# Plain float32 in chunk 0's output product and chunk 1's P times V, w_out split one chunk later, other buffers and load order

## The chip, the cores and the metric

One Trainium2 chip, one of its cores. The metric is device microseconds of one launch on that core: the median of the runs, and beside it one execution under the hardware profiler.

## What is computed

Three layers one after the other, in float32. Sliding-window attention with a distance bias (4 sequences of 576 tokens, 8 heads of 64), a gated layer without activation, and a routed layer in which each of 2304 tokens goes to one of 8 experts:

```python
scores = scale * q @ k.T + bias          # window 128, causal
x = softmax(scores) @ v                  # then [2304, 512]
x = (x @ w_a) * (x @ w_b) @ w_out        # d_ff 1536
logits = x @ w_gate + modality_bias[modality_id]
e = argmax(logits); g = softmax(logits)[e]
out = g * (relu(x @ w1[e]) @ w2[e])
```

q and k are scaled up by about 5.3 and 5.4 and the gate's weights by 8. moe_w_a, moe_w_b and moe_w_out arrive as float64; the kernel reads their two 32-bit words and makes a float32 out of them with three bit operations on VectorE (DVE).

## The kernel before

Tokens are cut into 18 tiles of 128, grouped in seven chunks of 3, 2, 2, 3, 3, 3 and 2 tiles (`CH`, line 33). The gated layer runs chunk by chunk; within a chunk it takes 12 steps j, one for each 128 columns of d_ff. A step makes two products of 24 instructions (`mm_ab`, line 489), multiplies them into `gf` on DVE, and one step later adds the output product (`mm_out`, line 505) for each tile of the chunk into three PSUM banks. While chunk c runs, attention for chunk c+1 is worked off between its products, an item being one tile of one pair of heads; a pair's loads are issued by `a_load` (line 141) and its operands made by `a_prep_q`, `a_prep_k`, `a_prep_v`.

Most products are split: each float32 operand is held as a rounded part and a remainder (type float32r), made by one cast on ScalarE (ACT) and one subtraction on DVE, and three terms replace one product. Plain float32 is used where `S32` (scores of chunks 0 and 1) and `V32` (probabilities times V, chunk 0) say so. With plain float32 the normalisation of the probabilities is put off to the eviction of the product (`pv_ev`), and the result must be turned by a transpose (`pv_tr`); the split form (`pv6_mm`) gives it turned already.

Chunk 0 has an order written out by hand. Its attention runs first (lines 739 to 832, under `manual_schedule`), with the float64 conversion of weight blocks 0 and 1 in between (`conv_step`). Then `slot0` (line 954) is one step of chunk 0 together with the conversion of block j+2 of w_a and w_b, of block j+1 of w_out, and with chunk 1's attention items. In it `wo_jobs` converts a w_out block, splits it and writes the split to DRAM (`wo_d`, line 481); all later chunks fetch that back (`wo_fetch`, line 485). Outside the hand-made part a planner orders each engine's instructions by priority and by its own model of when they are ready, SP's queue of transfers included.

Routing of a chunk's tokens happens in the first steps of the next: `rd_fetch` loads gate rows, `rd_dot` makes dot products on DVE, `rd_fin` writes the rows to `x2d`. `x2_init` (line 846) fills the rows of `x2d` that are not routed yet with zeros. After chunk 6 the experts run.

Buffers are rings named by tag: `asb` (two), `gf` (one), `g` (two), `wo` (four), `x2` (three), `x2T` (one).

Of the kernel before, what the change touches and what calls it, by code (L numbers as in the profile page):

```python
# [21 lines left out]
def attn_moe_moe2(ctx: ExitStack, tc, q, k, v, moe_w_a, moe_w_b, moe_w_out, modality_id,  # L22
# [39 lines left out]
    CJ = 3  # L62
    CA = 1
    QPB = 1
    EVD = 1
    PJ = 5
    KDE = (1,)
    V6 = (1, 2, 3, 4, 5, 6)
    S32 = (0, 1)
    V32 = (0,)  # L70

    const = ctx.enter_context(tc.tile_pool(name="const", bufs=1))
    rt = ctx.enter_context(tc.tile_pool(name="rt", bufs=2))
# [261 lines left out]
                                 start=(b == 0), stop=(b == 1))  # L335

    def pv_ev(it):
        it.o = at.tile([P, 2, D], F32, tag="uy"[(it.a.hp * it.a.nt + it.t) % 2], bufs=1, name="u")
        for h in range(2):
            if it.a.c == 0 and EVD:  # L340
                nc.vector.tensor_scalar(out=it.o[:, h], in0=it.po[:, h, 0:D],
                                        scalar1=it.mx[:, 6 + h:7 + h], scalar2=None, op0=ALU.mult)
                continue
            nc.scalar.activation(out=it.o[:, h], in_=it.po[:, h, 0:D], func=AF.Copy,
                                 scale=it.mx[:, 6 + h:7 + h])
# [77 lines left out]
    def f64_ops(rv, key, put):  # L423
        st = []

        def one():
            f = m1.tile([P, 4 * P], U32, name="f64f", **(dict(tag="x2T", bufs=1) if key == "o" else dict(tag="x2", bufs=X2B)))
            st.append(f)
            nc.vector.tensor_scalar(out=f, in0=rv[:, :, 1], scalar1=3, scalar2=0x3FFFFFFF,
                                    op0=ALU.logical_shift_left, op1=ALU.bitwise_and)  # L430

        def two():
            nc.vector.scalar_tensor_tensor(out=st[0], in0=rv[:, :, 1], scalar=0xC0000000, in1=st[0],  # L433
                                           op0=ALU.bitwise_and, op1=ALU.bitwise_or)
# [30 lines left out]
    WOQ = 0  # L465
    WOB = 4
    wo_d = dram.tile([NJ, P, 2, DM], F32, name="wo_d")
    wo_t = {}

    def wo_load(j):  # L470
        r = m1.tile([P, DM, 2], U32, tag="wo", bufs=WOB, name="wor")
        nc.sync.dma_start(out=r.rearrange("p a b -> p (a b)"), in_=moe_w_out.bitcast(U32)[j * P:(j + 1) * P, :])
        wraw["o", j] = r

    def wo_jobs(j):
        fs = []

        def sp():
            wo_t[j] = m1.tile([P, 2, DM], F32R, tag="wo", bufs=WOB, name="wo")
            f64_split(fs[0], wo_t[j], nc.vector)  # L480
            nc.sync.dma_start(out=wo_d[j], in_=wo_t[j].bitcast(F32))

        return f64_ops(wraw.pop(("o", j)), "o", fs) + [("s", sp)]

    def wo_fetch(j):
        wo_t[j] = m1.tile([P, 2, DM], F32R, tag="wo", bufs=WOB, name="wo")
        (nc.scalar if WOQ else nc.sync).dma_start(out=wo_t[j].bitcast(F32), in_=wo_d[j])

    def mm_ab(c, j, m, part=None):
        n = CH[c] * P  # L490
# [197 lines left out]
    def consts_load():  # L688
        nc.sync.dma_start(out=wg, in_=w_gate.rearrange("(k p) e -> p k e", p=P))
        nc.sync.dma_start(out=mb.rearrange("p m e -> p (m e)"),  # L690
                          in_=modality_bias.rearrange("m (o e) -> o (m e)", o=1).partition_broadcast(P))
        mid_i = cl[0] = m1.tile([P, NT, 2], I32, tag="asb", bufs=2, name="mid_i")
        nc.sync.dma_start(out=mid_i.rearrange("p t w -> p (t w)").rearrange("p (t w) -> p t w", w=2),
                          in_=modality_id.bitcast(I32).rearrange("(t p w) -> p t w", p=P, w=2))

    def consts_ap():
        cl[1] = tinit = m1.tile([P, TI * TW], I32, tag="asb", name="tinit")
# [25 lines left out]
    def consts_b():  # L723
        mid = rt.tile([P, NT], F32, tag="vt", bufs=1, name="mid")
        nc.gpsimd.tensor_copy(out=mid, in_=cl[0][:, :, 0])
        tb = m1.tile([P, NT * (E + 2)], F32, tag="asb", name="tb")
# [11 lines left out]

    with tc.manual_schedule():
        if WU:  # L740
            wz = m1.tile([P, 2 * P], BF16, tag="asb", bufs=2, name="wz")
            nc.vector.memset(wz.bitcast(F32), 0.0)
            wps = ps_at.tile([P, 2 * P], F32, tag="att", name="ps_w")
            for _ in range(WU):
                nc.tensor.matmul(wps, lhsT=wz[:, 0:P], rhs=wz, start=True, stop=True)
        for h in range(H):
            nc.vector.memset(qscale[64 * (h % 2):64 * (h % 2) + 64, h // 2:h // 2 + 1], 0.125 * 2.0 ** (h + 1))
        new_xr(0)
        a_loads(n0 - 1)
# [91 lines left out]
    def upto(w, f, g):  # L841
        while cur[w] < min(g, len(items)):
            f(cur[w])
            cur[w] += 1

    def x2_init():
        zrow = m1.tile([P, DM + 1], F32, tag="x2", bufs=X2B, name="zrow")
        nc.gpsimd.memset(zrow, 0.0)
        for i in range(C0[NC - 2 if NC - 2 in RD else NC - 1], NT + 1):
            nc.sync.dma_start(out=x2d[i * P:(i + 1) * P, :], in_=zrow)  # L850
# [95 lines left out]

    queued = []

    hold = []

    def cum0(j):
        return ((j + 1) * NP * CH[1] + NJ - 1) // NJ

    def slot0(j):
# [10 lines left out]
                with tc.high_priority(offset=HP0):  # L965
                    a_pv(live.pop(g))

        dq(hold, "s")
        hold.clear()
        dq(jw[:4], "d")  # L970
        psa = mm_ab(c, j, 0, None if j else 1)
        asb = m1.tile([P, MT * P], F32, tag="asb", bufs=2, name="asb")
        nc.scalar.copy(out=asb[:, :n], in_=psa[:, :n])
        if act:
            c1, hp1, t1 = items[g + 2]
# [7 lines left out]
                score_inv(sg)  # L983
                score_nrm(sg)
        psb = mm_ab(c, j, 1)
        gf = m1.tile([P, MT * P], F32, tag="gf", bufs=1, name="gf")
        nc.vector.tensor_tensor(out=gf[:, :n], in0=psb[:, :n], in1=asb[:, :n], op=ALU.mult)
        if last:
            V()
            x_split(1)  # L990
        gt = m1.tile([P, 2, MT * P], F32R, tag="g", bufs=2, name="g")
        nc.scalar.copy(out=gt[:, 0, :n], in_=gf[:, :n])
        (nc.gpsimd if j in GLP else nc.vector).tensor_tensor(out=gt[:, 1, :n], in0=gf[:, :n], in1=gt[:, 0, :n], op=ALU.subtract)
        if act:
# [12 lines left out]
    pend = None
    for c in range(NC):
        n = CH[c] * P
        for j in range(NJ):  # L1010
# [21 lines left out]
            if c == NC - 1 and j == EJ:
                assert cur["o"] == len(items)
# [302 lines left out]
```

## Time and profile before

| | us |
|---|---|
| median of 3 runs | 855.36 (854.55 to 856.16) |
| the profiled execution | 856.61 |
| its span, first to last instruction | 854.9 |
| mean granted TensorE clock | 0.988 |
| TensorE busy (PE) | 812.0, 95% |
| weight loads busy (PEld) | 740.3, 87% |
| VectorE (DVE) / ScalarE (ACT) / GpSimd (POOL) | 570.6 / 437.7 / 187.8 |

Times in the rows are microseconds unless marked ns. PE's busy time includes the latency of pipelined instructions, so a busy PE need not be at its peak. SPq is SyncE's queue, which issues nearly all transfers, in order. A digit of the busy line is the busy share of one fortieth of the span in tenths.

### The profile page before, as it was taken

The page shows a single profiled execution, that of the slowest core. Times are in us where ns is not written, and L with a number is a line of the kernel's source. Part 1 is how long each engine was busy: PE and PEld are TensorE (multiplying, and loading weights), DVE is VectorE, ACT ScalarE, POOL GpSimd, SP SyncE. Part 2 cuts the span into 40 slices and gives each one's busy share as a digit, 9 for nine tenths or more (in the row PEclk, how much of TensorE's full clock was granted, in tenths as well). Part 3 has the DMA queues.
Part 4 walks back from the last instruction along what each step waited for, and adds up shares of the span by engine and source line. Part 5 has one row for each costly group of instructions (what it writes and reads, how often), then busy time and mean ns, then how long its engine had stood idle before and what let it go on. Part 6 is the DMA issues. An engine that isn't in the chain of part 4 may idle for free.

```text
span 854.9 us, 14384 instructions
## 1 busy us (share of the span) xinstructions
PE 812.0 (95%) x4806; PEld 740.3 (87%) x4806; DVE 570.6 (67%) x1732; ACT 437.7 (51%) x1153; POOL 187.8 (22%) x245
## 2 busy tenths in 40 slices
PE   7889877999999999999999999999999999999994
PEld 5779766889899989999999999999988998989893
DVE  6999999896796797557955594368375544447420
ACT  5756674653756766566546642232245443546420
POOL 4413214022122222221222121100033130114001
PEclk8989999999999999999999999999999999999998
DMA  9994434478876556343544244647328564549201
GB/s 268 355 405 160 132 103 142 174 233 220 192 220 193 155 152 203 111 127 95 173 142 131 69 139 137 185 148 236 98 102 303 200 196 137 169 127 303 99 32 39
DMA packets 66274, 145.50 MB, mean 170 GB/s; under 512 B 11951, under 2 KB 32079, under 8 KB 66192
## 3 DMA queue, kind: packets, MB, share of 16 engines
q1 hardware_dynamic: 62576, 134.64, 51.1%
q0 software_dynamic: 3616, 9.86, 3.3%
q8 instruction: 40, 0.66, 0.3%
q14 instruction: 42, 0.34, 0.1%
HBM read 125.63 MB, written 19.11 MB: 169 GB/s over the span
## 4 chain that ended last, share of the span: by engine, by line
PE 71%; issue 8%; DVE 7%; DMA 6%; ACT 4%; POOL 2%; SPq 1%; POOLq 0%; ACTq 0%; DVEq 0%
PE ps_ab L498 29%; PE acc L512 14%; PE ps_y L1088 8%; PE ps_h L1105 8%; PE ps_o L369 4%; PE ps_s L247 2%; DMA wraw<-in_moe_w_a 1%; PE ps_p L297 1%; DMA kr<-in_k 1%; PE ps_s L243 1%; DMA qr<-in_q 1%; POOL out L1095 1%; DMA wo<-wo_d 1%; DVE wab L445 1%; DVE f64f L433 1%
## 5 line engine op out<-in xcount | busy, mean ns | idle before, releaser
L498 PE MATMUL ps_ab<-xr,wab 128*128 128x384 f32 (+1 forms) x2016 | 339.6, 317 | 7.0 <-ACT asb L1049 1.9
L498 PEld LDWEIGHTS ps_ab<-xr,wab 128*128 128x128 f32 x2016 | 308.9, 189 | 19.1 <-ACT wab L444 4.5
L512 PE MATMUL acc<-wo,g 128*128 128x512 f32 x648 | 174.1, 399 | 4.9 <-DVE wo L445 2.0
L512 PEld LDWEIGHTS acc<-wo,g 128*128 128x128 f32 x648 | 115.5, 188 | 23.9 <-DVE wo L445 3.0
L311 POOL TENSOR_SCALAR_AFFINE_SELECT pt<-pc 128x512 fp32r<-128x512 f32 (+1 forms) x72 | 57.2, 794 | 322.8 <-DVE pc L309 215.9
L1088 PE MATMUL ps_y<-w2s,h 128*128 128x512 f32 x456 | 109.7, 394 | 0.0
L1105 PE MATMUL ps_h<-xT,w1s 128*128 128x384 f32 x576 | 104.1, 337 | 0.0
L1105 PEld LDWEIGHTS ps_h<-xT,w1s 128*128 128x128 f32 x576 | 99.7, 188 | 1.1 <-issue 0.5
L1088 PEld LDWEIGHTS ps_y<-w2s,h 128*128 128x128 f32 x456 | 84.2, 188 | 16.7
L579 DVE CUSTOM_DVE_ANT_0 junk<-x,wgt 128x512 f32<-128x512 f32 x128 | 91.5, 715 | 7.7 <-DMA wgt<-in_wgt 4.6
L271 ACT ACTIVATE p<-p,mx 128x128 f32<-128x128 f32 x144 | 56.7, 396 | 30.2 <-DVE mx L261 29.6
L1056 ACT CAST g<-gf 128x256 fp32r<-128x256 f32 (+1 forms) x72 | 33.1, 459 | 62.8 <-DVE gf L1053 61.0
L1049 ACT COPY asb<-ps_ab 128x256 f32<-128x256 f32 (+1 forms) x72 | 30.6, 425 | 65.0 <-PE ps_ab L498 64.5
L1053 DVE TENSOR_TENSOR gf<-ps_ab,asb 128x256 f32<-128x256 f32 (+1 forms) x72 | 35.0, 486 | 41.8 <-PE ps_ab L498 37.1
L369 PE MATMUL ps_o<-pt,vv 128*128 128x256 f32 x360 | 56.6, 290 | 1.7 <-POOL pt L311 1.1
L313 POOL TENSOR_SCALAR_AFFINE_SELECT pt<-pc 128x512 fp32r<-128x512 f32 (+1 forms) x72 | 57.1, 792 | 0.0
L862 DVE TENSOR_TENSOR w2s<-wr,w2s 128x1024 fp32r<-128x1024 f32 x24 | 29.4, 1226 | 39.7 <-ACT w2s L861 39.5
L369 PEld LDWEIGHTS ps_o<-pt,vv 128*128 128x128 f32 x360 | 50.0, 189 | 4.1 <-POOL pt L311 1.4
L862 DVE TENSOR_TENSOR w1s<-wr,w1s 128x1024 fp32r<-128x1024 f32 x28 | 34.3, 1225 | 24.0 <-ACT w1s L861 24.0
L1095 POOL DMA_INDIRECT out<-y,idx x19 | 22.8, 1203 | 119.9 <-ACT y L1094 118.1
L284 ACT ACTIVATE p<-p,mx 128x128 f32<-128x128 f32 x120 | 41.5, 394 | 13.0 <-DVE mx L276 12.2
L1108 ACT ACTIVATE h<-ps_h 128x384 fp32r<-128x384 f32 x48 | 23.5, 492 | 47.0 <-PE ps_h L1105 47.0
(204 smaller groups left out, 1066.0 us busy)
## 6 DMA issues: line engine op xcount, KB each, us to landing
wo<-wo_d SPq DMA_DIRECT2D x72, 512.0 KB, 3.8
wr<-in_moe_w SPq DMA_DIRECT2D x56, 512.0 KB, 4.1
wgt<-in_wgt SPq DMA_DIRECT2D x24, 512.0 KB, 4.2
wraw<-in_moe_w_a SPq DMA_DIRECT2D x12, 512.0 KB, 8.9
wraw<-in_moe_w_b SPq DMA_DIRECT2D x12, 512.0 KB, 8.2
wor<-in_moe_w_out SPq DMA_DIRECT2D x12, 512.0 KB, 4.8
wo_d<-wo SPq DMA_DIRECT2D x12, 512.0 KB, 2.8
kr<-in_k SPq DMA_DIRECT2D x24, 256.0 KB, 4.2
```

The costliest lines, as they stand in the source:

```text
L271: nc.scalar.activation(out=it.p[:, h, :], in_=it.p[:, h, :], func=AF.Exp, bias=it.mx[:, 2 + h:3 + h], scale=-1.0, accum_out=it.mx[:, 4 + h ...
L284: nc.scalar.activation(out=it.p[:, h, :], in_=it.p[:, h, :], func=AF.Copy, scale=it.mx[:, 6 + h:7 + h])
L311: nc.gpsimd.affine_select(out=it.pt[:, :, 0], in_=pc, pattern=pat + [[-1, P]], base=0, channel_multiplier=1, compare_op=ALU.is_gt, fill=0.0)
L313: nc.gpsimd.affine_select(out=it.pt[:, :, 1], in_=pc, pattern=pat + [[1, P]], base=0, channel_multiplier=-1, compare_op=ALU.is_ge, fill=0.0)
L369: nc.tensor.matmul(it.po, lhsT=a.vv[:, t + b, r].rearrange("p h d -> p (h d)"), rhs=it.pt[:, :, b, s, :], start=(i == 0), stop=(i == 5))
L498: nc.tensor.matmul(ps[:, :n], lhsT=w[:, m, r, kk * P:(kk + 1) * P], rhs=xr[:, s, kk, :n], start=(idx == 0), stop=(idx == len(terms) - 1))
L512: nc.tensor.matmul(acc[c, t], lhsT=g[:, r, t * P:(t + 1) * P], rhs=w[:, s, :], start=(j == 0 and idx == 0), stop=(j == NJ - 1 and idx == 2))
L579: nc.vector.tensor_tensor_reduce(out=junk, in0=x2[:, 0:DM], in1=wgt[:, k], scale=1.0, scalar=0.0, op0=ALU.mult, op1=ALU.add, accum_out=lgr ...
L862: nc.vector.tensor_tensor(out=dst[:, 1], in0=srcw, in1=dst[:, 0], op=ALU.subtract)
L1053: nc.vector.tensor_tensor(out=gf[:, :n], in0=psb[:, :n], in1=asb[:, :n], op=ALU.mult)
L1088: nc.tensor.matmul(pss[t], lhsT=h[:, r, f, t * P:(t + 1) * P], rhs=W2[f // 2][:, s_, f % 2, :], start=(f == 0 and i == 0), stop=(f == 7 an ...
L1105: nc.tensor.matmul(ps, lhsT=W1[f // 2][:, r, kk, (f % 2) * P:(f % 2 + 1) * P], rhs=xT[:, s_, kk, :], start=(kk == 0 and i == 0), stop=(kk ...
```

## The change

Chunk 0's output product takes `gf` and w_out as they are, in plain float32. So in chunk 0 the split of g and that of w_out go. The converted w_out block goes to DRAM as plain float32 (`wo_f`); chunk 1 fetches it from there, splits it (`wo_split`), uses it and writes the split to `wo_d` for the later chunks. `V32` takes chunk 1 in: its probabilities stay plain float32, are normalised at the eviction, and a transpose is added. In chunk 0's attention one of the two evictions of an item goes from DVE to ACT. In SP's order weight block 0 now stands ahead of pairs 2 and 3 of chunk 0. The zero rows are written one block per step from step 5 of chunk 3, instead of six at step 2 of chunk 1. Buffers: `asb` has one instead of two; the modality table is loaded into `gf`, the bias table's scratch lies in `x2T`; the attention output `u` lies in `g` or `x2T`; the float32 w_out block lies in `wo`.

```diff
-    V32 = (0,)
+    V32 = (0, 1)
     def pv_ev(it):
-        it.o = at.tile([P, 2, D], F32, tag="uy"[(it.a.hp * it.a.nt + it.t) % 2], bufs=1, name="u")
+        it.o = m1.tile([P, 2, D], F32, name="u", **(dict(tag="x2T", bufs=1) if it.a.c else dict(tag="g", bufs=2)))
         for h in range(2):
-            if it.a.c == 0 and EVD:
+            if it.a.c == 0 and h == 0:
                 nc.vector.tensor_scalar(out=it.o[:, h], in0=it.po[:, h, 0:D],
...
-            f = m1.tile([P, 4 * P], U32, name="f64f", **(dict(tag="x2T", bufs=1) if key == "o" else dict(tag="x2", bufs=X2B)))
+            f = m1.tile([P, 4 * P], U32, name="f64f", **(dict(tag="wo", bufs=WOB) if key == "o" else dict(tag="x2", bufs=X2B)))
...
+    class WoOps(list):
+        def append(self, f):
+            wo_t[self.j] = f
+            nc.sync.dma_start(out=wo_f[self.j], in_=f)
     def wo_jobs(j):
-        fs = []
-        def sp():
-            wo_t[j] = m1.tile([P, 2, DM], F32R, tag="wo", bufs=WOB, name="wo")
-            f64_split(fs[0], wo_t[j], nc.vector)
-            nc.sync.dma_start(out=wo_d[j], in_=wo_t[j].bitcast(F32))
-        return f64_ops(wraw.pop(("o", j)), "o", fs) + [("s", sp)]
+        return f64_ops(wraw.pop(("o", j)), "o", WoOps(j))
+    def wo_fetch(j, c):
+        if c > 1:
             wo_t[j] = m1.tile([P, 2, DM], F32R, tag="wo", bufs=WOB, name="wo")
+            nc.sync.dma_start(out=wo_t[j].bitcast(F32), in_=wo_d[j])
+        else:
+            wo_s[j] = at.tile([P, DM], F32, tag="wos", bufs=2, name="wos")
+            nc.sync.dma_start(out=wo_s[j], in_=wo_f[j])
+    def wo_split(j):
+        f, w = wo_s.pop(j), wo_t[j]
+        nc.scalar.copy(out=w[:, 0], in_=f)
+        nc.vector.tensor_tensor(out=w[:, 1], in0=f, in1=w[:, 0], op=ALU.subtract)
+        nc.sync.dma_start(out=wo_d[j], in_=w.bitcast(F32))
...
         for t in range(CH[c]):
+            if c == 0:
+                nc.tensor.matmul(acc[c, t], lhsT=g[:, t * P:(t + 1) * P], rhs=w, start=(j == 0), stop=(j == NJ - 1))
+                continue
...
-        a_loads(n0 - 1)
+        a_loads(CH[0])
         qq_zero(pairs[0, 0])
         make_masks(lambda: a_preps(0))
+        wab_load(0)
+        a_loads(n0 - 1)
         for hp_ in range(1, NP):
             qq_zero(pairs[0, hp_])
         consts_load()
-        wab_load(0)
...
     def slot0(j):
-        dq(hold, "s")
-        hold.clear()
-        asb = m1.tile([P, MT * P], F32, tag="asb", bufs=2, name="asb")
+        asb = m1.tile([P, MT * P], F32, tag="asb", bufs=1, name="asb")
-        gf = m1.tile([P, MT * P], F32, tag="gf", bufs=1, name="gf")
+        gf = m1.tile([P, MT * P], F32, tag="g", bufs=2, name="gf")
-        gt = m1.tile([P, 2, MT * P], F32R, tag="g", bufs=2, name="g")
-        nc.scalar.copy(out=gt[:, 0, :n], in_=gf[:, :n])
-        (nc.gpsimd if j in GLP else nc.vector).tensor_tensor(out=gt[:, 1, :n], in0=gf[:, :n], in1=gt[:, 0, :n], op=ALU.subtract)
+        if last:
+            wo_fetch(0, 1)
+            wo_fetch(1, 1)
-        return c, j, gt, wo_t[j]
+        return c, j, gf, wo_t[j]
...
-            if c == 1 and j == 2:
+            if c == 3 and (j == 5 or j > 5 and zr):
                 x2_init()
...
             upto('o', do_pv, g - OG)
+            if c == 1:
+                wo_split(j)
+                if j + 2 < NJ:
+                    wo_fetch(j + 2, c)
```

## Rows read from the trace of the kernel before

**Rows 1.** The page's busy tenths in 40 slices of the span, for VectorE.

```profile
DVE  6999999896796797557955594368375544447420
```

**Rows 2.** Table by stretch: length, busy time (instructions) by engine, clock, DMA share, GB/s.

```profile
0.00:45.60 45.60, 34.58 (x195) 28.29 (x196) 37.42 (x174) 27.47 (x93) 19.97 (x60) 0.90 0.99 318
45.60:159.40 113.80, 99.74 (x528) 87.76 (x529) 109.62 (x268) 67.01 (x183) 28.61 (x28) 0.98 0.52 177
159.40:223.70 64.30, 62.23 (x446) 57.23 (x446) 50.47 (x181) 35.58 (x110) 12.72 (x15) 1.00 0.79 223
```

**Rows 3.** The same table for 15.6 to 22.4 and for stretches of the slots.

```profile
15.60:22.40 6.80, 5.40 (x19) 4.76 (x20) 6.19 (x28) 2.90 (x9) 2.20 (x7) 0.50 1.02 399
...
45.60:55.30 9.70, 8.64 (x36) 7.58 (x36) 8.35 (x25) 4.51 (x13) 0.61 (x2) 0.79 1.03 398
55.30:87.50 32.20, 32.14 (x179) 29.95 (x180) 31.73 (x81) 20.30 (x59) 8.70 (x10) 1.00 0.63 222
87.50:145.80 58.30, 45.58 (x248) 38.56 (x246) 56.49 (x142) 36.84 (x102) 18.37 (x16) 1.00 0.43 136
```

**Rows 4.** VectorE's timeline in chunk 0's attention: start, length, instruction, idle before it.

```profile
16.04 0.43 DVE L429 TENSOR_SCALAR f64f<-wraw 128x512 uint32<-128x512 uint32 x1 [4.84 <-DMA wraw<-in_moe_w_a]
...
22.51 0.47 DVE L341 TENSOR_SCALAR u<-ps_o,mx 128x64 f32<-128x64 f32 x2
```

**Rows 5.** The chain of waits before 60 us: start, length, what.

```profile
9.98 6.04 DMA wraw<-in_moe_w_a
...
17.45 1.71 PE ps_s L243 x4
...
24.00 0.87 PE ps_s L243 x4
...
25.09 0.84 PE ps_o L334 x8
25.93 0.12 PE ps_ot L351
...
42.58 9.77 DMA qr<-in_q
```

**Rows 6.** The chain of waits of the whole span, three undisturbed groups of split products.

```profile
343.14 1.44 PE ps_o L369 x12
...
397.33 4.17 PE ps_ab L498 x24
401.51 2.10 PE acc L512 x9
```

**Rows 7.** Groups by line and shape, 45.6 to 159.4, VectorE: busy, mean ns, idle before.

```profile
L445 DVE TENSOR_TENSOR wo<-f64f,wo 128x512 fp32r<-128x512 f32 x10 | 7.6, 755 | 0.4 <-ACT wo L444 0.3
...
L993 DVE TENSOR_TENSOR g<-gf,g 128x384 fp32r<-128x384 f32 x11 | 6.0, 547 | 0.0
...
L309 DVE TENSOR_TENSOR pc<-ps_p,pc 128x256 fp32r<-128x256 f32 x12 | 4.9, 412 | 1.5 <-ACT pc L308 1.5
...
L226 DVE TENSOR_TENSOR vv<-vr,vv 128x384 fp32r<-128x384 f32 x6 | 3.7, 619 | 0.0
```

**Rows 8.** The same groups for TensorE's products.

```profile
L498 PE MATMUL ps_ab<-xr,wab 128*128 128x384 f32 x288 | 58.0, 350 | 4.6 <-ACT wab L444 1.7 <-DVE f64f L437 1.7 <-DVE wab L445 0.9
L512 PE MATMUL acc<-wo,g 128*128 128x512 f32 x99 | 26.6, 400 | 2.1 <-DVE wo L445 2.0
L369 PE MATMUL ps_o<-pt,vv 128*128 128x256 f32 x66 | 11.3, 299 | 1.7 <-POOL pt L311 1.1 <-DVE pc L309 0.6
L243 PE MATMUL ps_s<-kk,qq 128*128 128x256 f32 x28 | 7.6, 396 | 0.0
```

**Rows 9.** The table by stretch, first half of chunk 1.

```profile
159.40:192.60 33.20, 31.13 (x218) 28.15 (x218) 29.23 (x87) 20.53 (x60) 5.88 (x6) 1.00 0.71 227
```

**Rows 10.** What SP's queue waited for, whole span: us in total, times, longest.

```profile
SPq L481 <- DVE wo L445: 21.6, 7, 8.8
```

**Rows 11.** SP's timeline, 199 to 224: the zero rows' writes.

```profile
206.70 3.07 SPq L850 DMA_DIRECT2D x2d<-zrow  x6
```

**Rows 12.** The chain of waits, 180 to 240: a load of k.

```profile
221.76 10.10 DMA kr<-in_k
```

More of the change, by code (lines that the diff above doesn't have):

```diff
@@ L64, in attn_moe_moe2 @@
     QPB = 1
-    EVD = 1
     PJ = 5
@@ L467, in attn_moe_moe2 @@
     wo_d = dram.tile([NJ, P, 2, DM], F32, name="wo_d")
+    wo_f = dram.tile([NJ, P, DM], F32, name="wo_f")
     wo_t = {}
@@ L473, in wo_load, with __init__ @@
         wraw["o", j] = r
+    class WoOps(list):
+        def __init__(self, j):
+            self.j = j
+        def append(self, f):
+            wo_t[self.j] = f
+            nc.sync.dma_start(out=wo_f[self.j], in_=f)
     def wo_jobs(j):
-        fs = []
-        def sp():
+        return f64_ops(wraw.pop(("o", j)), "o", WoOps(j))
+    wo_s = {}
+    def wo_fetch(j, c):
+        if c > 1:
             wo_t[j] = m1.tile([P, 2, DM], F32R, tag="wo", bufs=WOB, name="wo")
-            f64_split(fs[0], wo_t[j], nc.vector)
-            nc.sync.dma_start(out=wo_d[j], in_=wo_t[j].bitcast(F32))
-        return f64_ops(wraw.pop(("o", j)), "o", fs) + [("s", sp)]
-    def wo_fetch(j):
-        wo_t[j] = m1.tile([P, 2, DM], F32R, tag="wo", bufs=WOB, name="wo")
-        (nc.scalar if WOQ else nc.sync).dma_start(out=wo_t[j].bitcast(F32), in_=wo_d[j])
+            nc.sync.dma_start(out=wo_t[j].bitcast(F32), in_=wo_d[j])
[7 more added lines that the diff above has]
+        nc.sync.dma_start(out=wo_d[j], in_=w.bitcast(F32))
     def mm_ab(c, j, m, part=None):
@@ L691, in consts_load @@
                           in_=modality_bias.rearrange("m (o e) -> o (m e)", o=1).partition_broadcast(P))
-        mid_i = cl[0] = m1.tile([P, NT, 2], I32, tag="asb", bufs=2, name="mid_i")
+        mid_i = cl[0] = m1.tile([P, NT, 2], I32, tag="gf", bufs=1, name="mid_i")
         nc.sync.dma_start(out=mid_i.rearrange("p t w -> p (t w)").rearrange("p (t w) -> p t w", w=2),
@@ L696, in consts_ap @@
     def consts_ap():
-        cl[1] = tinit = m1.tile([P, TI * TW], I32, tag="asb", name="tinit")
+        cl[1] = tinit = m1.tile([P, TI * TW], I32, tag="asb", bufs=1, name="tinit")
         nc.gpsimd.iota(tinit, pattern=[[0, TI * TW]], base=N, channel_multiplier=1)
@@ L725, in consts_b @@
         nc.gpsimd.tensor_copy(out=mid, in_=cl[0][:, :, 0])
-        tb = m1.tile([P, NT * (E + 2)], F32, tag="asb", name="tb")
+        tb = m1.tile([P, NT * (E + 2)], F32, tag="x2T", bufs=1, name="tb")
         mm1 = tb[:, 0:2 * NT].rearrange("p (m t) -> p m t", m=2)
@@ L740, in attn_moe_moe2 @@
         if WU:
-            wz = m1.tile([P, 2 * P], BF16, tag="asb", bufs=2, name="wz")
+            wz = m1.tile([P, 2 * P], BF16, tag="asb", bufs=1, name="wz")
             nc.vector.memset(wz.bitcast(F32), 0.0)
@@ L844, in upto @@
             cur[w] += 1
+    zr = []
     def x2_init():
[L847 to L850, printed above, removed]
+        if not zr:
+            zrow = m1.tile([P, DM + 1], F32, tag="x2", bufs=X2B, name="zrow")
+            nc.gpsimd.memset(zrow, 0.0)
+            zr.extend((zrow, i) for i in range(C0[NC - 2 if NC - 2 in RD else NC - 1], NT + 1))
+        zrow, i = zr.pop(0)
+        nc.sync.dma_start(out=x2d[i * P:(i + 1) * P, :], in_=zrow)
+        return bool(zr)
     SP = [mybir.EngineType.SP]
@@ L947, in attn_moe_moe2 @@
     queued = []
-    hold = []
     def cum0(j):
@@ L1003, in slot0 @@
         a_preps(n0 + cum0(j) + PJ - 1)
-        hold.extend(jo)
-        return c, j, gt, wo_t[j]
+        return c, j, gf, wo_t[j]
     pend = None
@@ L1024, in attn_moe_moe2 @@
                     wo_load(j + 2)
-            else:
-                wo_fetch(j)
+            elif c > 1:
+                wo_fetch(j, c)
             a_loads(g + (LD if c else LD0))
@@ L1047, in attn_moe_moe2 @@
             psa = mm_ab(c, j, 0)
-            asb = m1.tile([P, MT * P], F32, tag="asb", bufs=2, name="asb")
+            asb = m1.tile([P, MT * P], F32, tag="asb", bufs=1, name="asb")
             nc.scalar.copy(out=asb[:, :n], in_=psa[:, :n])
@@ L1059, in attn_moe_moe2 @@
                 mm_out(*pend)
+            if c == 1:
+                wo_t[j] = m1.tile([P, 2, DM], F32R, tag="wo", bufs=WOB, name="wo")
             pend = (c, j, gt, wo_t[j])
             upto('o', do_pv, g - OG)
+            if c == 1:
+                wo_split(j)
+                if j + 2 < NJ:
+                    wo_fetch(j + 2, c)
             a_preps(g + 1)
@@ L1197, in s_gather @@
     def s_gather(ov):
-        idx = m1.tile([P, 1], I32, tag="asb", bufs=2, name="idx")
+        idx = m1.tile([P, 1], I32, tag="asb", bufs=1, name="idx")
         nc.sync.dma_start(out=idx, in_=tab[bass.ds(ov, P), 0:1])
```

## The prediction

> **What bounds the kernel now.** I read the page first: VectorE (DVE) is full in the first eight fortieths of the span, and nearly idle later [rows 1]. A table by stage then gives the limits. Up to 45.6 us chunk 0's attention runs; from 45.6 to 159.4 us chunk 0's twelve expert slots, with chunk 1's attention between them; from 159.4 to 223.7 us chunk 1's twelve steps [rows 2]. In the slots DVE is busy 109.6 of 113.8 us (96%), TensorE (PE) 99.7 and ScalarE (ACT) 67.0. In chunk 1 PE is busy 62.2 of 64.3 and DVE 50.5.
>
> PE's busy time covers the pipeline's latency too, so I count its work by passes. On the undisturbed chain 24 products of 384 columns take 4.17 us (0.174 each), 9 of 512 columns 2.10 (0.234), 12 of 256 columns 1.44 (0.120) [rows 6]; these are split (fp32r) operands, one pass each. Plain float32 shows twice as many instructions as products: 4 of 256 columns in 0.87 us (0.217 each), 8 of 64 columns in 0.84 (0.105 each) [rows 5]. In the slots PE runs 288, 99, 66 and 28 of these four larger kinds [rows 8], and 47 more instructions (528 in all, rows 2) that I price at 0.12: 50.1 + 23.2 + 7.9 + 6.1 + 5.6 = 92.9 us in 113.8. So DVE is the limit of this stage, but not evenly. From 55.3 to 87.5 us both engines are full; from 87.5 to 145.8 DVE has 56.5 of 58.3 us, PE 45.6 [rows 3]. The first slot, 45.6 to 55.3, is limited by neither: the clock averages 0.79, and the DMA engines are at 1.03 [rows 3].
>
> In the attention before it DVE waits 4.84 us, until 16.04, for the first raw weight block; that transfer was issued only at 9.98 [rows 4, 5].
>
> **Start: block 0 loaded ahead of pairs 2 and 3.** Its two transfers move ahead of two pairs and three constants in SP's queue. Six loads of 192 KB stand before it instead of twelve and more, so it should land about when DVE first asks, at 11.2. Term: -4.8 (bounds 0, if the order does not come out so, and -4.8). From 15.6 to 22.4 us, right after the engines had stood still in that wait, the granted clock is 0.50, that is 1.2 instead of 2.4 GHz, and a score group takes 1.71 us instead of 0.87 [rows 3, 5]. The 6.8 us hold up to three such groups, 2.5 us dearer, but DVE is busy for 6.2 of them; I take -1.0 (0 to -2.5). Pairs 2 and 3 come later by 1 MB, at the 399 GB/s shown there 2.6 us; two pairs of work lie before them, so I take 0 (to +2.6).
>
> **Start: half of each eviction leaves DVE.** Two evictions take 0.47 us [rows 4]; one of two goes to ACT, 12 x 0.235 = 2.8, and chunk 1's first V split (0.6) goes. ACT has 18 us free here [rows 2]. Where a step is held by PE (0.87 + 0.84 and three transposes of 0.12 for an item, rows 5) the gain is hidden: I take -2.5 (0 to -3.4).
>
> **Start: what is late next.** The next late thing is visible: a load of q for chunk 1, issued at 42.58, lands at 52.34 and ends an ACT wait on the chain [rows 5], with the DMA engines full. The bytes ahead of it are nearly the same after the change. If its place in SP's order stays, it eats all that the start gains (8.3); if the planner moves it up with the step that frees its buffer, nothing. I take +2.5 (0 to +8.3), nearer to the second, because its buffer is freed by that step.
>
> **Slots: DVE.** Removed: 11 subtractions of g (6.0), 10 of w_out (7.6), 8 of the 12 on pc (chunk 1 has four pairs of two tiles; 8 x 0.412 = 3.3), 3 on vv (3 x 0.62 = 1.9) [rows 7]. 109.6 - 18.8 = 90.8. ACT loses the casts beside them and chunk 1's normalisation, and gains two small evictions and a copy per item; at 67.0 of 113.8 it hides them. GpSimd's selects take half the width, and cost nothing where hidden.
>
> **Slots: PE.** A plain float32 output product replaces three split ones. Its two instructions at 512 columns are not in the trace; from 0.217 at 256 columns I take 0.432 each: 0.864 against 3 x 0.234 = 0.702, or +0.162; 33 in this window, +5.3 us. Lower bound: two passes at the split price, 0.468, a gain of 7.7 us; excluded as a value, since 256 columns already cost 0.217 against 0.120. Upper bound: two passes at twice 0.234, 0.936, +7.7 us. P times V for chunk 1 becomes 8 passes (0.84) and a transpose (0.12) for 6 split ones (0.72): +0.24 an item, +1.9. PE: 92.9 + 5.3 + 1.9 = 100.1.
>
> At 256 columns a plain product takes 0.434, and four split passes would take 0.48 [rows 5, 6]. The Trainium skill (FP8 and Floating Point Precision, TensorE Precision Notes) counts true FP32 as 4 passes through the array, which speaks against this change, as the split needs 3. By that count a product at 512 columns would be 4 x 0.234 = 0.936, the slots 2.4 us longer and the forecast near 847; the trace agrees but for 10%, and I go by its row.
>
> **Slots: the sum.** DVE falls to 90.8, PE rises to 100.1: PE becomes the bound. The first slot's 36 instructions [rows 3] are 24 products, 8 plain score passes and 4 small ones, 6.1 us by the prices above; it loses 3.6 us beyond that, which I keep: 103.7. In the stretch from 87.5 DVE's 56.5 lose their share by time of the 18.8 (9.6), PE's 45.6 gain theirs of the 7.2 (3.7): 46.9 and 49.3, so the two are level and must wait for each other in turn; I add 1.8 for each, the idle that DVE shows there now: 107.3. Term: 113.8 to 107.3, -6.5 (-13.7 if PE's work alone counts; -0.9 if PE waits 0.7 at each of the eight new transposes, which need ACT's eviction first and hold the slot's products behind them).
>
> **Chunk 1.** The split of w_out comes here: an ACT copy (0.62) and a DVE subtraction (0.755 [rows 7]) per step, with a 512 KB write that SP issues only after the subtraction, and a 256 KB fetch in place of 512. Queued behind that write are the fetch for step j+2 and the k, q and v loads of the next chunk; the out-product of the next step waits for the subtraction. On ACT the copy waits for the fetch, with the next evictions and exponentials behind it. In the first half DVE is busy 29.2 of 33.2 [rows 9]: six more make 33.8, over the stretch by 0.6, and any delay comes in order. In the second half there is room. I take +2.5 (-1, as PE loses about 2 us now, to +7).
>
> **Zero rows.** Six writes of 256 KB leave 206.7 to 209.8 us, and 12 us later loads of k take 10.10 us [rows 11, 12]. One per step in chunk 3 costs nothing there. I take -1.0 (-2.6 to +0.5; the w_out writes put a net 3 MB into this chunk where the zero rows put 1.5). The single asb buffer waits for a product that the PSUM bank's next user awaits anyway: 0 (to +2). The bias table's scratch and the modality load: 0, as SP reaches that load long after the mask scratch it now shares is free.
>
> **Sum.** -4.8 - 1.0 - 2.5 + 2.5 - 6.5 + 2.5 - 1.0 = -10.8. The profiled execution took 856.61 us (span 854.9, 1.7 around it); 845.8 by the sum. The median of the runs is 855.36, 1.25 lower, so I forecast 844.6.
>
> **Rivals.** (a) The front is held by transfers, or the planner leaves SP's order as it is: the start's 8.3 are lost or eaten, 2.5 given back less. 844.6 + 5.8 = 850.4. For it: DMA share 0.99 up to 45.6 and 1.03 after it [rows 2, 3]. Against: up to 45.6 DVE idles 8.2 us, 4.84 of them in the one wait that the change attacks [rows 2, 4].
> (b) All covers hold: transfers move up with the prologue (-2.5), slots reach 103.7 (-3.6), chunk 1 absorbs the split (-2.5): 836.0. For it: DVE's room in chunk 1's second half. Against: both engines level.
> (c) Slower: chunk 1's split. SP holds the write of w_out until DVE subtracts, with loads behind it. In the slots that wait came 7 times in 12, 21.6 us in all, 3.1 each, at most 8.8 [rows 10]. If the subtraction falls behind routing's dot products in DVE's queue by more than a step (5.3 us), the next out-product, and PE, stand still. Six steps at 3.1, 18.6 in place of 2.5, give 860.7. It decides from five of the twelve steps on: 842.1 + 15.5 = 857.6. Against: PE lost only 2 us in that half so far.
> (d) The gains and the losses meet: PE's additions fall on the slots that are full now, with (a): about 855.
>
> **How the numbers follow.** A difference of 0.2% (1.7 us) is about what a measurement of this kernel can tell. Forecast, 839 to 850: 0.56. (a) 0.12; (b) 0.13; (c) 0.11; (d) 0.08. Range: from (b) with its bounds, 833, to 854.5, leaving out (c) and part of (d). Faster: forecast, (a) and (b), 0.81; same 0.07 and slower 0.12 from (d) and (c).
>
> **What would show it.** Right: no wait for wraw near 11 us; the attention ends near 38 to 40; slots of chunk 0 with PE above 95% and DVE below it; output products as two instructions of about 0.43 spacing; chunk 1 at 65 to 68 us; no 10 us loads near 220. Wrong: an ACT wait for q of over 5 us in slot 0; a pass near 0.47 or 0.23; PE idle in chunk 1 ended by the subtraction of w_out; PE idle before the transpose of chunk 1's outputs.

## The result and the profile after

The changed kernel takes 844.98 us (median of 4 runs, 843.65 to 846.12) against 855.76 for the kernel before beside it: 0.9872, interval 0.9846 to 0.9898. The forecast was 844.6. The profiled execution took 843.99 us with a span of 842.2, 12.7 less than before. By stage (a chunk begins with its first step product):

| us | start | chunk 0 slots | chunk 1 | 2 | 3 | 4 | 5 | 6 | rest |
|---|---|---|---|---|---|---|---|---|---|
| before | 45.6 | 113.7 | 64.4 | 68.6 | 96.9 | 92.9 | 82.5 | 52.2 | 238.0 |
| after | 41.2 | 102.4 | 64.2 | 68.6 | 98.7 | 93.8 | 82.8 | 52.2 | 238.3 |

The total came out as forecast; its parts did not. The start gave 4.4 us instead of 5.8, the slots 11.3 instead of 6.5, chunk 1 cost nothing instead of 2.5, and chunk 3, where the zero rows were to cost nothing, lost 1.8.

First the page's digits for VectorE in the kernel after, against [rows 1]: the full stretch at the front has holes.

```profile
DVE  8989995987875976658865683377376444447420
```

The table by stretch of the kernel after (length; busy us of PE, PEld, DVE, ACT, POOL with instructions; clock, DMA share, GB/s): the start, the slots, chunk 1, chunk 3; then the first slot alone and the inner part of the start. It answers [rows 2, 3].

```profile
0.00:41.20 41.20, 35.10 (x196) 26.63 (x196) 35.27 (x163) 28.54 (x101) 20.46 (x60) 0.98 0.96 295
41.20:143.60 102.40, 102.40 (x519) 84.62 (x519) 92.08 (x237) 53.60 (x158) 17.45 (x28) 0.98 0.61 211
143.60:207.80 64.20, 62.32 (x444) 56.77 (x443) 53.25 (x183) 39.91 (x112) 11.32 (x14) 1.00 0.70 219
276.40:375.10 98.70, 95.08 (x565) 88.50 (x564) 67.78 (x230) 61.01 (x183) 22.67 (x31) 1.00 0.59 156
...
41.20:51.10 9.90, 9.90 (x48) 9.16 (x47) 7.44 (x24) 3.87 (x12) 2.39 (x5) 0.75 1.02 409
16.00:38.00 22.00, 19.11 (x116) 14.50 (x115) 19.76 (x86) 17.37 (x65) 11.11 (x26) 1.00 1.03 336
```

In the slots PE is busy all 102.40 us, DVE 92.08: the bound has passed from DVE to PE. In chunk 3 PE stands idle for 3.6 us, where it was 1.4 before. From 16 to 38 us the granted clock is 1.00, where part of it was 0.50 before.

DVE's timeline of the kernel after at the point of [rows 4]: the first raw weight block now costs a wait of 0.61 us at 11.38, where it cost 4.84 at 16.04.

```profile
11.38 0.55 DVE L428 TENSOR_SCALAR f64f<-wraw 128x512 uint32<-128x512 uint32 x1 [0.61 <-DMA wraw<-in_moe_w_a]
```

The waits of the start after, of ACT and of PE (us in total, times, longest): the eviction given to ACT waits for DVE's half of the same result, and PE's transposes wait for ACT.

```profile
ACT u L343 <- DVE u L340: 6.1, 7, 1.3
...
PE ps_ot L350 <- ACT u L343: 1.5, 3, 0.8
```

Groups by line and shape after, 41.2 to 143.6 for PE and (last line) chunk 1 for DVE, against [rows 7, 8]: 66 instructions of the plain output product stand where 99 split ones stood, and the split of w_out is on DVE in chunk 1.

```profile
L511 PE MATMUL ps_ab<-xr,wab 128*128 128x384 f32 x288 | 62.5, 362 | 0.0
L524 PE MATMUL acc<-f64f,gf 128*128 128x512 f32 x66 | 30.8, 594 | 0.0
L242 PE MATMUL ps_s<-kk,qq 128*128 128x256 f32 x28 | 8.3, 412 | 0.0
L333 PE MATMUL ps_o<-vv,pt 128*128 128x64 f32 x64 | 8.3, 268 | 0.0
...
L499 DVE TENSOR_TENSOR wo<-wos,wo 128x512 fp32r<-128x512 f32 x11 | 7.6, 690 | 2.6 <-ACT wo L498 1.8 <-DMA wo_d<-wo 0.8
```

The chain of waits of the kernel after: four plain passes of 512 columns, and in chunk 3 a load of gate rows, which stands where [rows 12] had a load of k.

```profile
56.48 1.72 PE acc L524 x4
...
292.67 9.77 DMA wgt<-in_wgt
```

SP's timeline after, in chunk 3: the six zero writes are one group still.

```profile
282.42 4.06 SPq L871 DMA_DIRECT2D x2d<-zrow  x6
```

### The profile page after: what moved, and what is told of

It reads as the page before. It is cut to its first block, busy times and chain, and to the rows that moved or that the text cites. A ratio compares the mean times of both kernels' runs of the same rounds, so it can differ in the third digit from the quotient of the medians.

```text
span 842.2 us, 14322 instructions
## 1 busy us (share of the span) xinstructions
PE 816.2 (97%) x4794; PEld 735.7 (87%) x4794; DVE 554.5 (66%) x1696; ACT 430.3 (51%) x1141; POOL 176.5 (21%) x245
## 4 chain that ended last, share of the span: by engine, by line
PE 79%; issue 7%; DVE 5%; ACT 4%; DMA 3%; POOL 1%; SPq 0%; POOLq 0%; ACTq 0%; DVEq 0%
PE ps_ab L511 33%; PE acc L528 13%; PE ps_y L1111 8%; PE ps_h L1128 8%; PE ps_o L368 4%; PE acc L524 4%; PE ps_s L246 3%; PE ps_p L296 1%; DMA wgt<-in_wgt 1%; PE ps_o L333 1%; POOL out L1118 1%; PE ps_s L242 1%; PE ps_t L933 1%; DVE junk L595 1%; ACT p L270 1%
## 5 line engine op out<-in xcount | busy, mean ns | idle before, releaser
L511 PE MATMUL ps_ab<-xr,wab 128*128 128x384 f32 (+1 forms) x2016 | 348.1, 319 | 3.3 <-DVE xr L414 1.1
L528 PE MATMUL acc<-wo,g 128*128 128x512 f32 x540 | 143.9, 397 | 0.0
L310 POOL TENSOR_SCALAR_AFFINE_SELECT pt<-pc 128x512 fp32r<-128x512 f32 (+1 forms) x72 | 51.2, 711 | 320.8 <-DVE pc L308 158.3
L528 PEld LDWEIGHTS acc<-wo,g 128*128 128x128 f32 x540 | 96.6, 188 | 15.3
L270 ACT ACTIVATE p<-p,mx 128x128 f32<-128x128 f32 x144 | 56.8, 396 | 29.2 <-DVE mx L260 28.7
L312 POOL TENSOR_SCALAR_AFFINE_SELECT pt<-pc 128x512 fp32r<-128x512 f32 (+1 forms) x72 | 51.5, 715 | 0.0
L368 PE MATMUL ps_o<-pt,vv 128*128 128x256 f32 x312 | 47.5, 288 | 0.0
L1074 DVE TENSOR_TENSOR g<-gf,g 128x256 fp32r<-128x256 f32 (+1 forms) x72 | 38.2, 530 | 12.4 <-ACT g L1073 12.4
L1132 DVE SCALAR_TENSOR_TENSOR h<-ps_h,h 128x384 fp32r<-128x384 f32 x48 | 26.3, 554 | 28.8 <-ACT h L1131 28.8
```

Of the source, the lines that this page charges most:

```text
L270: nc.scalar.activation(out=it.p[:, h, :], in_=it.p[:, h, :], func=AF.Exp, bias=it.mx[:, 2 + h:3 + h], scale=-1.0, accum_out=it.mx[:, 4 + h ...
L310: nc.gpsimd.affine_select(out=it.pt[:, :, 0], in_=pc, pattern=pat + [[-1, P]], base=0, channel_multiplier=1, compare_op=ALU.is_gt, fill=0.0)
L312: nc.gpsimd.affine_select(out=it.pt[:, :, 1], in_=pc, pattern=pat + [[1, P]], base=0, channel_multiplier=-1, compare_op=ALU.is_ge, fill=0.0)
L368: nc.tensor.matmul(it.po, lhsT=a.vv[:, t + b, r].rearrange("p h d -> p (h d)"), rhs=it.pt[:, :, b, s, :], start=(i == 0), stop=(i == 5))
L511: nc.tensor.matmul(ps[:, :n], lhsT=w[:, m, r, kk * P:(kk + 1) * P], rhs=xr[:, s, kk, :n], start=(idx == 0), stop=(idx == len(terms) - 1))
```

## The experiments

Each kernel has a ratio to the kernel before, run beside it on the same chip, with its 95% interval; stage times are of the profiled execution. The kernel before took 855.76 to 857.22 us beside the four groups of runs, so medians of two groups compare to about 1.5 us. The first four undo one part of the changed kernel each, the next two do one part alone, and so on.

### Load order undone: e1_load_back

```diff
-        a_loads(CH[0])
+        a_loads(n0 - 1)
         qq_zero(pairs[0, 0])
         make_masks(lambda: a_preps(0))
-        wab_load(0)
-        a_loads(n0 - 1)
...
         consts_load()
+        wab_load(0)
```

> The changed kernel with weight block 0 loaded behind pairs 2 and 3 and the constants again, as before the change. Theory (the load order is what the start gained, 45.6 to 41.2 us): DVE waits some 4 us for wraw near 11 us again, the clock falls right after it, the slots begin near 45.5, and the whole takes 4 to 5 us longer, near 849. Rival (transfers hold the front: what the start gains is waited for later, at the load of q in slot 0): the slots begin at 45.5 but slot 0 gets shorter by as much, and the whole stays within 1.5 us of 845.

848.84 us, 0.992 (0.9894 to 0.9947): 3.9 us slower than the changed kernel. Its DVE timeline shows the wait again:

```profile
18.01 0.43 DVE L428 TENSOR_SCALAR f64f<-wraw 128x512 uint32<-128x512 uint32 x1 [6.80 <-DMA wraw<-in_moe_w_a]
```

The start is 48.3 us instead of 41.2, with the clock low (0.50) for 10.2 us of it from 16.9; the slots give 1.3 back and chunk 3 gives 1.5. So in the changed kernel the load order is worth 7.1 us at the start, where the prediction had 5.8, and about 4 in the whole.

### Zero rows paced: e2_zero_paced

`wo_dma` holds the step's fetch of w_out.

```diff
         zrow, i = zr.pop(0)
-        nc.sync.dma_start(out=x2d[i * P:(i + 1) * P, :], in_=zrow)
+        with tc.issue_after(wo_dma[0].ins):
+            nc.sync.dma_start(out=x2d[i * P:(i + 1) * P, :], in_=zrow)
```

> The changed kernel with each zero-row write tied in SP's order behind that step's fetch of w_out, so that the six writes stand one per step in chunk 3 instead of together at 282 to 286 us. Theory (the burst delays the gate rows' load, 9.8 us at 292.7, DVE waits for it and PE idles): chunk 3 falls from 98.7 to about 96.9, the step of 12 us near 303 goes back to 8 to 9, the whole near 843. Rival (chunk 3's loss has nothing to do with the burst, it comes from routing's dot products in DVE's queue): chunk 3 stays at 98 to 99 and the whole at 845.

840.5 us, 0.9814 (0.9792 to 0.9835). SP's timeline has the writes apart, each behind a fetch of w_out:

```profile
308.01 0.38 SPq L873 DMA_DIRECT2D x2d<-zrow  x1
308.59 0.32 SPq L492 DMA_DIRECT2D wo<-wo_d  x1
308.96 0.48 SPq L873 DMA_DIRECT2D x2d<-zrow  x1
...
318.26 0.32 SPq L873 DMA_DIRECT2D x2d<-zrow  x1
```

DVE's wait for gate rows in chunk 3 goes with it. The first line is the changed kernel's table of waits, the second that of this one:

```profile
DVE junk L595 <- DMA wgt<-in_wgt: 4.7, 1, 4.7
```

```profile
DVE junk L596 <- DMA wgt<-in_wgt: 0.3, 1, 0.3
```

Chunk 3 takes 95.3 us instead of 98.7. So the loss there is the six writes in one group, ahead of the gate rows.

### P times V of chunk 1 split again: e3_pv_split

```diff
-    V32 = (0, 1)
+    V32 = (0,)
```

> The changed kernel with chunk 1's probabilities times V split again; the output product of chunk 0 stays plain. Theory (PE is the bound in chunk 0's slots now, and the plain form costs it 0.24 us an item): PE's work falls by 1.9 from 99.9, DVE's rises by about 5 from 92.1, both are full near 98: the slots take 101 to 104 us, the whole 844 to 847, so this part of the change is worth little by itself. Rival (DVE's relief is what counts, PE waits for it): the slots lengthen by the 5 us of DVE work, to 107, the whole near 850.

842.19 us, 0.9831 (0.9809 to 0.9852), an interval that just touches the changed kernel's: in the whole this part gains nothing there. The start is 1.8 us longer and the slots 1.1, chunk 1 is 2.2 shorter (62.0): at the end of chunk 1 the two kernels are 0.8 us apart, in favour of the changed one. What makes e3 the shorter lies behind, 1.9 us in chunk 3 and 0.9 in chunk 4, where this edit changes no product.

### Both evictions on DVE: e4_ev_dve

```diff
-            if it.a.c == 0 and h == 0:
+            if it.a.c == 0:
```

> The changed kernel with both evictions of an item of chunk 0 on DVE again. Theory (ACT's eviction waits for DVE's and lengthens the path from product to transpose, so the hand-over gained nothing): two on DVE take 0.47 in place of 0.27 + 0.32 in a row; the slots begin at 40 to 41.5 instead of 41.2, the whole within 1.5 us of 845. Rival (the handed-over eviction is a real gain of 2.5 us, as forecast): the slots begin near 43.7 and the whole takes 847 to 848.

841.88 us, 0.983 (0.9811 to 0.985). The start is 40.0 us instead of 41.2, with the whole eviction back on DVE: the hand-over to ACT did not gain 2.5 us, it lost 1.2. The rest of the difference lies outside the stage that the edit touches, 0.9 of it in chunk 3.

### Load order alone: f1_load_only

The diff of e1_load_back, the other way round, in the kernel before.

> The kernel before with the load order of the changed kernel alone: pairs 2 and 3 of chunk 0 behind weight block 0. Theory (the late weight block costs the start 4.8 us of waiting and a slow clock after it): the slots begin at 41 to 42 instead of 45.6 and the whole takes 851 to 852. Rival (DVE-bound slots and the saturated transfers take it back): slot 0 and 1 get longer, the whole is within 1.7 us of the kernel before.

856.77 us, 0.9998 (0.9988 to 1.0008). The rival held: nothing is left of it. The start is 41.6 us, 4.0 shorter, and the first slot 16.06 instead of 9.71. At the end of the slots the kernel is even 3.4 us behind (121.2 us of slots instead of 113.7); chunks 1 and 2 give 4.7 back (61.4 and 66.9), because PE idles there for 0.3 us instead of 3.8. Why it does is open. ACT's timeline, then PE's, say why: the split of q (`qq`) waits 5.95 us for its load, and behind it stand the probabilities that PE is to transpose next and the slot's first eviction (`asb`).

```profile
54.08 1.02 ACT L207 ACTIVATE qq<-qr,qscale 64x256 f32<-64x256 f32 x2 [5.95 <-DMA qr<-in_q]
...
56.50 0.46 ACT L974 COPY asb<-ps_ab 128x384 f32<-128x384 f32 x1
```

```profile
55.59 0.47 PE L297 MATMUL ps_p<-ident,p 128*128 128x128 f32 x1 [5.91 <-ACT p L284]
```

The slot in the table by stretch: 16 us, PE busy 10, clock 0.71.

```profile
41.60:57.70 16.10, 10.19 (x37) 8.94 (x37) 8.11 (x24) 4.51 (x13) 0.61 (x2) 0.71 1.03 403
```

### Output product alone: f2_out_only

The changed kernel without the other four edits: the split P times V, the old load order, both evictions on DVE, the zero rows in chunk 1 as before. Its w_out is still split in chunk 1.

> The kernel before with chunk 0's output product in plain float32, the split of w_out in chunk 1 and the buffers that this needs; load order, evictions, P times V of chunk 1 and zero rows as before. Theory (the slots' gain comes from this part, since it takes 13.6 us off DVE and puts 5.3 on PE): the slots fall from 113.7 to 102 to 105, the start stays at 45.6, the whole near 845 to 848. Rival (the gain needs both parts): the slots stay above 108 and the whole above 850.

844.32 us, 0.9853 (0.9835 to 0.987), as much as the whole change. Table by stretch, the slots and chunk 1:

```profile
45.80:149.30 103.50, 101.90 (x489) 82.31 (x489) 99.09 (x250) 57.19 (x166) 24.09 (x26) 0.97 0.56 188
149.30:211.00 61.70, 61.35 (x451) 57.03 (x450) 54.05 (x186) 39.37 (x114) 14.75 (x18) 1.00 0.86 233
```

Ten us come out of the slots. Chunk 1 carries the split of w_out and has PE busy 61.35 of 61.70 us: that split costs next to nothing.

### Zero rows back in chunk 1: f3_zero_back

`x2_init` writes all six again at one call.

```diff
...
-            if c == 3 and (j == 5 or j > 5 and zr):
+            if c == 1 and j == 2:
                 x2_init()
```

> The changed kernel with the zero rows written in chunk 1 again, six at once. Theory (the burst costs wherever loads are waited for): chunk 3 falls from 98.7 to about 97 as in the kernel before, chunks 1 and 2 grow from 132.8 by 1 to 2.5, since the writes of w_out lie there now; the whole within 1 us of 845. Rival (moving them out of chunk 1 was worth the 1.0 forecast, or more): the whole 846 or above with chunk 3 unchanged.

841.35 us, 0.9815 (0.9798 to 0.9831). Chunk 3 falls to 95.3, chunk 2 rises to 70.7. So taking the writes out of chunk 1 gains 2.1 us in chunk 2, and writing them in one group in chunk 3 costs 3.4: moving them was a loss as it was done.

### The good parts together: f4_combo

The changed kernel with the edits of e2, e3 and e4.

> The changed kernel with three things: zero rows tied one per step, both evictions on DVE, chunk 1's P times V split. Theory (the three effects lie in different stages: chunk 3 3.4 us, the start 1.2, chunks 3 to 5 1 to 2): the whole 837 to 839. Rival (they overlap, each gained by moving the same burst of loads in chunk 3): no better than 840.5.

838.35 us, 0.9786 (0.977 to 0.9802): the fastest of all. Stages: 40.4, then 104.0, 61.6, 69.1, 95.8, and from there as before. Alone, the three edits are worth 2.8 to 4.5 us each by the medians; together 6.6. It differs from f2_out_only by the load order and the paced zero rows, and 5.3 us of its 6.0 lie in the start. So the load order, which is worth 0 in the kernel before, is worth about 5 here; the next two runs ask why. In f4 ACT has two evictions ahead of the split of q, and the split waits where nobody needs it yet:

```profile
47.62 0.48 ACT L993 COPY asb<-ps_ab 128x384 f32<-128x384 f32 x1 [1.34 <-PE ps_ab L512]
...
50.57 0.48 ACT L993 COPY asb<-ps_ab 128x384 f32<-128x384 f32 x1 [1.02 <-DVE f64f L436]
...
53.74 1.03 ACT L206 ACTIVATE qq<-qr,qscale 64x256 f32<-64x256 f32 x2 [1.37 <-DMA qr<-in_q]
```

### Load order alone, split of q behind the first eviction: g1_load_q_behind

In slot 0 alone:

```diff
-        nc.scalar.copy(out=asb[:, :n], in_=psa[:, :n])
+        cp = nc.scalar.copy(out=asb[:, :n], in_=psa[:, :n])
...
+            with tc.issue_after(cp.ins):
+                a_preps(n0 + cum0(j) + PJ - 1)
```

> The kernel before with the load order alone, and in chunk 0's first slot ScalarE splits q of chunk 1's third pair behind the first eviction of the slot instead of ahead of two exponentials and that eviction. Theory (the load order gains 4 us at the start, and in the old kernel loses them in slot 0 only because the split of q, which waits for its load until 54.0, stands ahead of the eviction on ScalarE): the first eviction comes near 48 instead of 56.5, slot 0 falls from 16.06 to 11 to 13 us (the transposed probabilities and the next weight block still stand behind the split), total near 853, ratio 0.994 to 0.997. Rival (the transfers themselves hold slot 0, whatever the order on ScalarE): slot 0 stays near 16, total 856.8, ratio 1.000.

856.23 us, 1.0007 (0.9993 to 1.0022). The theory's slot came (9.00 us instead of 16.06), its gain did not: the second slot takes 12.87 us instead of 7.19. ACT's timeline, then PE's:

```profile
50.73 0.46 ACT L974 COPY asb<-ps_ab 128x384 f32<-128x384 f32 x1
55.52 1.02 ACT L207 ACTIVATE qq<-qr,qscale 64x256 f32<-64x256 f32 x2 [4.33 <-DMA qr<-in_q]
...
60.41 0.51 ACT L225 CAST vv<-vr 128x384 fp32r<-128x384 f32 x1 [2.30 <-DMA vr<-in_v]
60.83 0.51 ACT L993 CAST g<-gf 128x384 fp32r<-128x384 f32 x1
```

```profile
61.39 2.92 PE L512 MATMUL acc<-wo,g 128*128 128x512 f32 x6 [5.71 <-ACT g L993]
```

The same late loads (q, then v of chunk 1) hold ACT, and now the cast of g, without which the output product can't start, stands behind them. The place of the one split does not decide by itself.

### The fastest kernel, split of q ahead of the first eviction: g2_combo_q_ahead

In slot 0 alone, and no longer at that slot's end:

```diff
+            a_preps(n0 + cum0(j) + PJ - 1)
+            with tc.issue_after(pairs[1, 2].qi.ins):
+                nc.scalar.copy(out=asb[:, :n], in_=psa[:, :n])
```

> The mirror of it: the fastest kernel so far (f4_combo) with that split of q put ahead of slot 0's first eviction on ScalarE, nothing else. Theory (the place of the split decides): the eviction waits for q until about 54, slot 0 grows from 9.9 to about 15 us, total 838.4 + 4 to 5 = 842.5 to 843.5. Rival (place is of no weight, the changed kernel escapes by other means, its shorter work on VectorE or its transfers): 838.4 within 0.7.

845.79 us, 0.9886 (0.9869 to 0.9902). The span is 7.4 us longer than f4's, more than the theory's 4 to 5: 4.7 lie in the slots and 2.7 in chunk 1 (64.3 us). Slot 0 takes 15.24 us instead of 7.71. ACT's timeline, then PE's:

```profile
53.92 1.02 ACT L206 ACTIVATE qq<-qr,qscale 64x256 f32<-64x256 f32 x2 [2.94 <-DMA qr<-in_q]
54.97 0.48 ACT L998 COPY asb<-ps_ab 128x384 f32<-128x384 f32 x1
```

```profile
55.50 5.73 PE L512 MATMUL ps_ab<-xr,wab 128*128 128x384 f32 x19 [6.02 <-ACT asb L998]
```

q lands at the same time in f1, f4 and g2 (54.0, 53.7, 53.9). What differs is what stands behind its split on ACT.

### P times V alone: g3_pv_only

The kernel before with `V32 = (0, 1)`.

> The kernel before with plain float32 probabilities times V in chunk 1 alone (V32 with both chunks). Theory (VectorE is the limit of chunk 0's slots before, so what leaves it counts there, though it is worth nothing behind the output product): 5.2 us leave VectorE, 1.9 come to TensorE, of which the slots between 87.5 and 145.8, where VectorE was the limit, keep about half: slots 113.7 to 111, total near 853, ratio 0.996 to 0.998. Rival (as in e3_pv_split, a part that gains nothing, or costs TensorE's 1.9): 855.5 to 858, ratio 0.999 to 1.003.

850.49 us, 0.9934 (0.9912 to 0.9955), twice the theory's gain. Table by stretch, the slots:

```profile
45.90:153.80 107.90, 101.74 (x551) 92.68 (x552) 103.47 (x259) 63.04 (x173) 24.55 (x28) 0.95 0.56 193
```

DVE loses 6.1 us against [rows 2], and the slots 5.8: in the kernel before DVE was the limit, and each us off it counted. Behind the output product, where PE is the limit, the same edit is worth nothing in the whole (e3).

## Why the prediction was right, point by point

**Slots, passes: right.** A plain instruction of 512 columns takes 1.72 / 4 = 0.43 us, a product 0.86 (forecast 0.864). The stage's passes, 288, 66, 28 and 64 of the kinds above with 38 split ones of 256 columns and 35 small ones of the same view, come to 50.1 + 28.4 + 6.1 + 6.7 + 4.6 + 4.2 = 100.1 us, which is the forecast's figure. An estimate from the four passes that the Trainium skill (FP8 and Floating Point Precision, TensorE Precision Notes) counts for true FP32 gives 0.936 a product (4 x 0.234); the trace shows 0.86. DVE: forecast 90.8, measured 92.1.

**Slots, the sum: 4.9 us too pessimistic (107.3 against 102.4).** The step that failed is the addition for two level engines that wait for each other, 3.6 us in all. There is no such loss: slots two to twelve take 92.5 us, their passes 92.7, and the slots of 11 to 14 us of before are gone. The 3.6 us kept for the first slot were 2.5 (by the prediction's own prices its 36 instructions before come to 6.4 us, not 6.1, so 3.3 were to be kept): its passes come to 7.4 us, it took 9.9, and 2.4 of the difference are the 4.9 us it spends at the lower clock (it began in a low stretch of 6.8 us from 39.25).

**Start, load order: right in the changed kernel, 0 without the rest.** The wait fell by 4.2 us and the clock stays at 1.00 through 16 to 38 us. Measured at the end of the slots, it loses 3.4 us with the split output product (f1 against the kernel before) and gains 4.8 with the plain one (f4 against f2). Rival (a), a front held by transfers, is true of the old kernel (f1) and false of the new one. My reason for taking only 2.5 of the 8.3 us, that the load of q moves up with the start, was wrong: its issue is 42.58 before, 43.92 in f1, 43.99 in f4, and in the changed kernel it is 48.03, 5.5 us later than before. Even so it held nobody there, because the split of q comes on ACT behind two evictions and finds its load landed:

```profile
57.35 1.02 ACT L206 ACTIVATE qq<-qr,qscale 64x256 f32<-64x256 f32 x2
```

g2 shows what an eviction behind its split costs, and g1 that with the eviction ahead the cast of g is next. The plain output product has no cast of g: one of the things that stood behind the late q and v on ACT is gone, and the planner put the evictions ahead. That the missing cast by itself opens the way is argued from g1's row, not tried.

**Start, evictions: wrong sign.** The term counted DVE's 12 x 0.235 us and not the chain: two evictions on DVE took 0.47 [rows 4], one on each took 0.27 and then 0.32 in series, because ACT's half waits for DVE's. e4 gains 1.2 us of start by undoing it; with P times V split, f4's start is 2.6 us shorter than e3's.

**Chunk 1: too dear by 2.7 (forecast +2.5, measured -0.2).** The wait of rival (c) is there: SP stands ahead of the write of w_out for 27.7 us in 11 waits, the longest 5.3, 7.7 of it put down to the subtraction and the rest to the work queued ahead of it on DVE. But none of PE's waits in the chunk ends with the subtraction; these are all of them:

```profile
PE ps_ab L511 <- DVE gf L1070: 1.0, 2, 0.7
PE ps_s L246 <- ACT xf L374: 0.8, 1, 0.8
```

Chunk 1 takes 61.4 to 62.0 us in five kernels (e3, f1, f2, f4, g1) and about 64 in the others. The five have PE idle for 0.0 to 0.4 us in it, the others for 1.9 to 2.1. In e3, f2 and f4, besides, 6 plain passes of chunk 0's last output product (2.6 us) fall before the border of the stage instead of behind it, and 12 split ones (1.4 us) behind it, so a part of their shorter chunk 1 is a longer slot. What sets the idle time is the planner's order, and which part of it stays open. Chunk 4 goes by the same rule (92.9 with no idle time, 93.8 with 1.1).

**Zero rows: wrong sign (-1.0 forecast, +1.8 in chunk 3).** The gain that the term counted on was there. In the kernel before, the load of k [rows 12] holds ACT; behind its cast of k stand the split of q and the cast of g, and PE waits for that cast. The chain of waits, then PE's timeline:

```profile
231.95 1.05 ACT kk L191
...
234.17 0.41 ACT g L1056
...
234.63 1.20 PE acc L512 x4
```

```profile
234.63 1.20 PE L512 MATMUL acc<-wo,g 128*128 128x512 f32 x4 [1.57 <-ACT g L1056]
```

After the change PE idles for 0.4 us in chunk 2 instead of 1.7; the stage still takes 68.6, as 505 of PE's instructions fall into it instead of 494. What failed is the other half, that one block per step in chunk 3 costs nothing. The table by stretch of the kernel after has PE idle for 2.7 us around its load of gate rows:

```profile
292.00:304.00 12.00, 9.28 (x57) 8.48 (x56) 7.22 (x19) 3.52 (x11) 2.26 (x3) 1.00 1.02 236
```

The program's one block per step is not what is issued, since the planner reorders SP's queue; I named that as a rival for the load order, and not here. Paced, the writes cost next to nothing: chunk 3 takes 95.3 us in e2, and 95.3 in f3, which has no zero rows there.

**P times V: a part of the sum, never weighed alone.** By the sum's own figures it takes work from DVE, which has room after the output product's edit, and gives PE, the new bound, 1.9 us. The runs say the same: 5.5 us gained alone, and behind the output product 0.8 up to the end of chunk 1 and nothing in the whole.

So 844.6 was right by errors that cancel: -4.9 in the slots and -2.7 in chunk 1 against +1.4 at the start and +4.3 from the zero rows and the chunks behind them, -1.9 for the span; the medians agree better, since the profiled execution lies 1.0 under its own. Rival (b), with slots at 103.7 and an absorbed split, told these two stages better than the forecast; the zero rows and the evictions kept the kernel from its 836, and f4, without them, takes 838.35. Two of the signs set out beforehand missed by little: the attention ends at 41.2, not 38 to 40, and chunk 1 takes 64.2, not 65 to 68. The mechanism that carries the result, DVE as the limit of chunk 0 with PE close behind, was right: f2 shows it, with 10 us out of the slots from the output product alone.

## What to carry to other kernels

Work taken off a full engine counts only until the next engine is full: find the second limit by counting passes, and do not pay twice for edits that relieve the same one. A transfer that lands late costs what stands behind its first reader on that engine's queue, so an earlier start can be eaten whole, and an edit that removes an instruction from that queue can free it. Where a planner orders the queue, read the issued order in the trace before crediting a move, and tie a step to something that paces it.

## What the runs showed that was not expected

Two loads behind the same six zero writes, of k before (10.10 us) and of gate rows after (9.77 us), took the same time with the DMA engines full; the first cost PE 1.6 us by way of ACT's queue, the second 2.7 by way of DVE's. And a wait of about 6 us on PE is paid twice: in f1, g2 and g1 a stretch of 6.8 us at the lower granted clock (0.50, that is 1.2 instead of 2.4 GHz) begins at 54.1, 53.4 and 59.8, while PE stands idle for 5.9, 6.0 and 5.7 us. In f4, which has no such wait, the clock stays at 1.00 there.
